# Second mixing one step further behind the first: a fused attention and gated feed-forward kernel in fp32

## The chip, the core and the metric

The kernel runs on one core of one Trainium2 chip. A core has five engines with a queue of instructions each: TensorE (PE, with its weight loads PEld), VectorE (DVE), ScalarE (ACT), GpSimd (POOL) and SyncE (SP, which here only starts transfers). Each engine works through its queue in order and waits on semaphores for the others. The metric is the device time of one launch in microseconds (us); lower is better.

## What is computed

Attention with two mixings over the heads, then a gated feed-forward block. Batch 4, 12 heads, 448 tokens, head size 64, everything in fp32.

```
scores = scale * np.matmul(q, k.transpose(0, 1, 3, 2))
scores = np.einsum('bhij,hg->bgij', scores, w_pre)      # first mixing
scores = scores - np.max(scores, axis=-1, keepdims=True)
attn = np.exp(scores)
attn = attn / (np.sum(attn, axis=-1, keepdims=True) + 1e-09)
attn = np.einsum('bhij,hg->bgij', attn, w_post)         # second mixing
x = np.matmul(attn, v)
...
xn = x / rms * rms_g
g = xn @ w_gate
out = (g / (1 + np.exp(-g)) * (xn @ w_val)) @ w_out     # 1792 tokens, 768 -> 1536 -> 768
```

## The kernel before

The first part (function `part_a`) is the attention, a software pipeline written out by hand. The queries of a batch are cut into four chunks, 16 chunks in all (`NCHUNK`); a chunk is worked in 6 steps, the last of each batch in 5 (`PAIRS`), which makes `T` = 92 steps. `first[n]` is the first step of chunk n. One step t does, in this order of issue:

- the transfers and small jobs due at t (`jobs_at`), among them in the steps of chunk 4 the reading of the first raw feed-forward weights: `fetch_w` starts a transfer into a ring of tiles with the tag "wraw", `first_w` issues one of five VectorE operations (lines 513 to 517) or the store of the result to `wf`;
- the first mixing `premix(t)` (line 182, tile `sp`, PSUM, contraction over 60 rows, a pair of 64-row halves), its matmuls alternating with those of one product of q and k for a later chunk (`qk_mm`, line 134, tile `qk`);
- `rowmax(t)` on VectorE (line 189, tile `nm`) and `expo(t)` on ScalarE (line 196, tile `e`, two tiles a step, with their sums `s`);
- the second mixing `postmix(t-1)` of the step before (line 223, tile `pm`), whose weights are the tiles `e` and whose moving operand is `wn`;
- the due units of the product with v (`av_mm`, line 267, from the table `av_at`), 16 short matmuls each;
- the copies of qk out of PSUM into `st` (lines 154 and 156) and the transfers that spread `st` over the rows of `r` (line 173), then the copies of pm into `at_all` (line 236 on VectorE, 238 on ScalarE);
- `norm(t)`: two small VectorE operations (`t` line 203, `rp` line 205) and on GpSimd `wn` (line 208), the mixing weights divided by the sums.

So `postmix(t-1)` stands in TensorE's queue after the first mixing of step t, and needs `wn` of t-1, which VectorE and GpSimd finish at the end of step t-1. GpSimd also adds and squares the results of the product with v (lines 290 to 305, tiles `xt` and `sum`, one operation a step, more towards the end).

In the last steps and for a few steps behind T, `extra` takes work of the second part into the pipeline: it loads x and the first weights again (`x_load`, `w_load`), splits each into a high and a low part (`x_split`, lines 577 and 578; `w_split`, line 684 on ScalarE and 685 on GpSimd, tile `wl`), and issues the first products (`both`, lines 600 to 602). What it takes in a step is decided by a budget of us per engine, `left`, which is smaller in steps in which a product with v is copied out (`done`). GpSimd also makes three tiles `d` (`diagonals`, line 358), which TensorE spreads over the partitions (`psy`, line 368). The second part (`part_b`) then is products of 128 by 128 weights with 448 columns, one behind the other, and is not touched by the change.

Tiles with one tag share a ring of `bufs` places; a write into a place waits until all readers of what stood there are done.

Of the kernel before, what the change touches and what calls it, by code (L numbers as in the profile page):

```python
# [7 lines left out]
F32 = mybir.dt.float32  # L8
# [37 lines left out]
def attention_moe(ctx: ExitStack, tc, q, k, v, wpre, wpost, mask, ident, wgv, wo, rms_g, out):  # L46
# [144 lines left out]
    def expo(n, p):  # L191
        sm[n, p] = pe.tile([128, 2], F32, name="s", tag="s")
        et[n, p] = []
        for u, ps in enumerate(sps.pop((n, p))):
            e = pe.tile([128, S], F32, name="e", tag="e", bufs=4)
            nc.scalar.activation(e, ps[:, :S], AF.Exp, bias=nmx.pop((n, p, u)), accum_out=sm[n, p][:, u : u + 1])  # L196
            et[n, p].append(e)

    def norm(n, p):
        k_ = halves_of(n, p)  # L200
        s = sm.pop((n, p))[:, :k_]
        t = pe.tile([128, 2], F32, name="t", tag="t")[:, :k_]
        nc.vector.tensor_scalar(t, s, 1e-9, None, ALU.add)
        r = pe.tile([128, 2], F32, name="rp", tag="rp")[:, :k_]
        nc.vector.reciprocal(r, t)  # L205
        wn[n, p] = pe.tile([128, 2, HR], F32, name="wn", tag="wn")
        for u in range(k_):
            nc.gpsimd.tensor_scalar(wn[n, p][:, u], wk, r[:, u : u + 1], 1.0, ALU.mult, ALU.mult)  # L208

    def postmix(n, p):  # L210
        ps = banks(ps_m, "pm")
        e, w = et.pop((n, p)), wn.pop((n, p))
        for u in range(2):
            u_ = min(u, len(e) - 1)
            for c in range(JC):
                for m in range(2) if c < JC - 1 else (u,):
                    j = min(2 * c + m, S // JT - 1) * JT
                    for v_ in range(2):
                        sl = slice(64 * v_, 64 * v_ + HR)
                        at_ = u * (JC - 1) + c if c < JC - 1 else JB - 1  # L220
                        o = ps[v_][64 * m : 64 * m + JT, : JB * HR].rearrange("p (s a i) -> p s a i", s=2, a=JB)
                        w_ = w[sl, u_].rearrange("p (s i) -> p s i", s=2)
                        nc.tensor.matmul(o[:, :, at_], e[u_][sl, j : j + JT], w_, start=True, stop=True)  # L223
        pm[n, p] = ps
# [155 lines left out]
    for i, a in enumerate([(n, hp) for n in range(1, NCHUNK) for hp in range(H // 2)][AHEAD:]):  # L380
        qk_at[i].append(a)
    for blk, ns in enumerate(BLOCKS):
        lo = first[ns[-1] + 1] + 1
        hi = first[ns[-1] + (3 if ns[-1] < 13 else 2)] + 1
        units = [(blk, i, part) for i in range(H // 2) for part in ((0, 1) if len(ns) > 1 else (None,))]
        for i, a in enumerate(units):
            t = lo + i * (hi - lo) // len(units)
            av_at[t].append(a)
            if ns[-1] % NC == NC - 1 and a[2] == 1:
                jobs_at[t + 1].append((load_v, ns[-1] // NC + 1, heads_of(blk)[a[1]]))  # L390

    def job(t, f, *a):
        jobs_at[t].append((f, *a))

    for n in range(NCHUNK):
        b, c = divmod(n, NC)
        if n > 2:
            for i in range(2):
                job(6 * n - 16 + 3 * i, load_q, n, 3 * i)
        for hp in range(H // 2):  # L400
            if n == 0:
                job(5 + 2 * hp, load_v, 0, heads_of(0)[hp])
        if n == 4:
            for i in range(4 * 7):
                job(first[n] + 4 + i, lambda i: first_w(i), i)
            for p in range(4):
                job(first[n] + 7 * p, lambda p: fetch_w(p), p)
    for t, todo_ in enumerate(list(qk_at)):
        for n, hp in todo_:
            if n % NC == NC - 1 and n + 1 < NCHUNK:  # L410
                job(t + 1, load_k, n // NC + 1, hp)
    for b in range(B - 1):
        t = first[NC * b + NC + 2] + (5 if b < B - 2 else 3)
        for i in range(17):
            last_at[t + max(i - 2, 0) // 3].append((sq_all, b, i))

    def part_a(extra):
# [29 lines left out]
        done = []  # L447
        for t in range(T + 24):
            def back(lag):
                return steps[t - lag] if 0 <= t - lag < T else None  # L450

            if t == first[NCHUNK - 1]:
                qk_ctx.close()
# [19 lines left out]
            if back(0):  # L473
                rowmax(*back(0))
                expo(*back(0))
            if back(1):
                postmix(*back(1))
            for a in av_at[t]:
                av_mm(*a)
            for a in qk_at[t][:1]:  # L480
                for j in range(2):
                    qk_evac(*a, j)
            if back(1):
                for v_ in range(2):
                    evac_a(*back(1), v_)
            if back(0) and t >= T - 2:
# [127 lines left out]
    conv = {}  # L614

    def fetch_w(p):
        raw = conv["raw", p] = pq.tile([128, 384, 2], I32, name="wraw", tag="wraw", bufs=3)
        src = wgv[0, :, 3 * p : 3 * p + 3].rearrange("p a f -> p (a f)").bitcast(I32)
        nc.sync.dma_start(raw.rearrange("p n t -> p (n t)"), src)

    def first_w(i):

        p, i = divmod(i, 7)
        if i < 5:
            if i == 0:
                conv["t"] = pq.tile([128, 2, 384], I32, name="wac", tag="wraw", bufs=3)
                conv[p] = to_f32(conv.pop(("raw", p)), *(conv["t"][:, j] for j in range(2)))
            conv[p][i]()
        elif i == 5:
            nc.sync.dma_start(wf[p // 2][:, (p % 2) * 384 : (p % 2) * 384 + 384], conv["t"][:, 1].bitcast(F32))  # L630
# [364 lines left out]
```

## Time and profile before

| | |
|---|---|
| time, median of 3 runs | 866.77 us (863.86, 866.77, 867.71) |
| the profiled execution | 866.41 us, its span 864.6 us |
| first steps to the last of the attention | about 21 to 346 us of the span |
| from there to the first product of the second part alone | 346 to 362 us |
| second part | 362.0 to 864.6 us |
| granted TensorE clock | 0.999 of full speed |

The span is what lies between the first and the last recorded instruction of the core; 1.8 us of the profiled time lie around it. A row of the profile names a line of the kernel, an engine, an operation and the tiles (out<-in), then how often, how long, and for how long the engine stood idle before it and what ended that. "issue" is idle time for which the profile shows no releaser. Matmuls overlap, and TensorE's busy share stays near 1 where short gaps between matmuls are covered by the modelled end of the one before; the gaps then show in the weight loads (PEld), which are issued in the same order.

### The profile page before, as it was taken

To read this page: it belongs to the slowest core of one execution; us is meant where nothing else is said; L and a number is where in the kernel's file an instruction comes from. 1 tells how busy PE (TensorE), PEld (TensorE's weight loads), DVE (VectorE), ACT (ScalarE), POOL (GpSimd) and SP (SyncE) were. 2 spreads that over 40 slices of the span, in tenths; PEclk is the share of its full clock that TensorE was granted. 3 is DMA by queue.
4 is the path that set the end of the run, shared out by engine and by line. 5 is a ranking of instruction groups with operands and counts; after the bars stand their busy time and mean duration, and the time that the engine had idled before them with its cause. 6 is when DMAs were issued, how large, how long until landed. Compare 5 with 4: busy or idle time off the path is not lost.

```text
span 864.6 us, 26550 instructions
## 1 busy us (share of the span) xinstructions
PE 827.3 (96%) x10900; PEld 710.8 (82%) x10900; DVE 600.4 (69%) x985; ACT 390.4 (45%) x869; POOL 437.6 (51%) x537
## 2 busy tenths in 40 slices
PE   7899999998899898999999999999999999999998
PEld 2556777777678686799999999999999999999997
DVE  5676787887677666778655858576668359978461
ACT  3677777777677676732211222222121235554310
POOL 7233455554555347935634646365356369573100
PEclk9999999999999999999999999999999999999999
DMA  7777678667756653744634535535354246664541
GB/s 203 202 229 206 202 226 237 213 196 220 223 156 178 184 165 111 231 155 118 215 100 153 139 119 154 179 98 170 105 180 138 64 134 195 201 189 134 170 129 64
DMA packets 77547, 144.53 MB, mean 167 GB/s; under 512 B 10495, under 2 KB 66845, under 8 KB 77427
## 3 DMA queue, kind: packets, MB, share of 16 engines
q1 hardware_dynamic: 72814, 129.19, 49.0%
q0 software_dynamic: 3648, 11.31, 4.8%
q10 hardware_dynamic: 965, 2.34, 0.8%
q8 instruction: 86, 1.41, 0.7%
q14 instruction: 34, 0.28, 0.1%
HBM read 72.03 MB, written 31.21 MB: 119 GB/s over the span
## 4 chain that ended last, share of the span: by engine, by line
PE 90%; DMA 3%; issue 3%; POOL 2%; DVE 1%; ACT 0%; ACTq 0%; SPq 0%; POOLq 0%; DVEq 0%
PE pm L223 9%; PE qk L134 8%; PE sp L182 7%; PE av L267 7%; PE pg L608 6%; PE pg L609 6%; PE pv L609 6%; PE pg L610 6%; PE pv L610 6%; PE pv L608 6%; PE po L610 6%; PE po L609 6%; PE po L608 6%; DMA r<-st 3%; POOL d L358 0%
## 5 line engine op out<-in xcount | busy, mean ns | idle before, releaser
L182 PE MATMUL sp<-r,wk_pre 64*64 64x448 f32 x720 | 162.7, 539 | 4.4 <-DMA r<-st 2.0
L134 PE MATMUL qk<-k,q 64*64 64x448 f32 x768 | 154.6, 560 | 5.9 <-DMA q<-in_q 4.1
L196 ACT ACTIVATE e<-sp,nm 128x448 f32<-128x448 f32 x180 | 114.4, 638 | 88.4 <-DVE nm L189 86.2
L223 PEld LDWEIGHTS pm<-wn,e 60*64 60x64 f32 x5152 | 110.1, 134 | 50.9 <-POOL wn L208 21.5
L189 DVE TENSOR_REDUCE nm<-sp 128x1 f32<-128x448 f32 x180 | 111.5, 622 | 56.2 <-PE sp L182 25.3
L208 POOL TENSOR_SCALAR wn<-wk,rp 128x60 f32<-128x60 f32 x180 | 55.8, 322 | 162.4 <-DVE rp L205 143.1
L223 PE MATMUL pm<-wn,e 60*64 60x60 f32 x5152 | 109.5, 220 | 18.0 <-issue 14.9
L267 PE MATMUL av<-at_all,v 64*64 64x240 f32 (+4 forms) x1728 | 95.1, 319 | 3.6 <-issue 3.6
L608 PE MATMUL pg<-x,wh 128*128 128x448 f32 x264 | 96.8, 367 | 0.0
L609 PE MATMUL pv<-x,wh 128*128 128x448 f32 x264 | 96.4, 365 | 0.0
L608 PE MATMUL pv<-x,wh 128*128 128x448 f32 x264 | 96.4, 365 | 0.0
L610 PE MATMUL pg<-x,wl 128*128 128x448 f32 x264 | 96.4, 365 | 0.0
L610 PE MATMUL pv<-x,wl 128*128 128x448 f32 x264 | 96.4, 365 | 0.0
L609 PE MATMUL pg<-x,wh 128*128 128x448 f32 x264 | 96.4, 365 | 0.0
L595 DVE TENSOR_TENSOR x<-hraw,x 128x448 fp32r<-128x448 f32 x84 | 91.6, 1137 | 6.8 <-ACT x L594 6.8
L609 PE MATMUL po<-x,fac 128*128 128x448 f32 x252 | 92.1, 365 | 0.0
L608 PE MATMUL po<-x,fac 128*128 128x448 f32 x252 | 92.0, 365 | 0.0
L610 PE MATMUL po<-x,fac 128*128 128x448 f32 x252 | 92.0, 365 | 0.0
L642 POOL TENSOR_TENSOR sg<-sg,u 128x448 f32<-128x448 f32 x36 | 48.1, 1335 | 83.0 <-DVE u L638 43.5
L637 ACT ACTIVATE sg<-g 128x448 f32<-128x448 f32 x48 | 27.4, 571 | 129.2 <-DVE g L636 118.6
L182 PEld LDWEIGHTS sp<-r,wk_pre 64*64 64x64 f32 x720 | 62.4, 133 | 22.2 <-issue 9.6
L638 DVE TENSOR_TENSOR u<-pv,ry 128x448 f32<-128x448 f32 x48 | 29.9, 623 | 69.1 <-PE pv L610 60.6
(118 smaller groups left out, 1709.9 us busy)
## 6 DMA issues: line engine op xcount, KB each, us to landing
r<-st SPq DMA_DIRECT2D x117, 210.0 KB
hraw<-td SPq DMA_DIRECT2D x84, 224.0 KB
wraw<-in_wgv SPq DMA_DIRECT2D x20, 768.0 KB
td<-keep SPq DMA_DIRECT2D x48, 224.0 KB
wraw<-in_wo SPq DMA_DIRECT2D x12, 768.0 KB
r<-st SPq DMA_DIRECT2D x44, 175.0 KB
v<-in_v SPq DMA_DIRECT2D x24, 256.0 KB
q<-in_q POOLq DMA_DIRECT2D x28, 192.0 KB, 5.1
```

The lines of the kernel that those rows point to most:

```text
L134: nc.tensor.matmul(ps[j][m, :S], qt[n][sl, hp, m], kt[n // NC, hp][sl], start=True, stop=True)
L182: nc.tensor.matmul(o, wk_pre[sl], rt[n][sl, 2 * p + v_], start=True, stop=True)
L189: nc.vector.tensor_reduce(t, ps[:, :S], AX.X, ALU.max, negate=True)
L196: nc.scalar.activation(e, ps[:, :S], AF.Exp, bias=nmx.pop((n, p, u)), accum_out=sm[n, p][:, u : u + 1])
L208: nc.gpsimd.tensor_scalar(wn[n, p][:, u], wk, r[:, u : u + 1], 1.0, ALU.mult, ALU.mult)
L223: nc.tensor.matmul(o[:, :, at_], e[u_][sl, j : j + JT], w_, start=True, stop=True)
L267: nc.tensor.matmul(x, vt[b, hp][sl, j, c_], a, start=(c_ == 0), stop=(c_ == JC - 1))
L595: nc.vector.tensor_tensor(lo, raw, hi.bitcast(F32), ALU.subtract)
L608: nc.tensor.matmul(ps, a, xh[:, kk], start=(kk == 0), stop=False)
L609: nc.tensor.matmul(ps, a, xl_[:, kk], start=False, stop=False)
L610: nc.tensor.matmul(ps, a2, xh[:, kk], start=False, stop=(kk == KT - 1))
L642: nc.gpsimd.tensor_tensor(h, sg, u, ALU.mult)
```

## The change

The second mixing of a step is issued two steps behind the first one, not one: `back(2)` where `back(1)` stood. After the last first mixing, in step T, both mixings that are left are issued one behind the other. The units of the product with v and the sums of squares (`sq_all`) go one step later with it, but for the last chunk. For this, six tiles `e` are kept in place of four. To make room, `t` and `rp` have three places in place of five, and the raw weights two in place of three, so that a raw tile is fetched every 9 steps, not every 7, each behind the store of the one before.

```
-            e = pe.tile([128, S], F32, name="e", tag="e", bufs=4)
+            e = pe.tile([128, S], F32, name="e", tag="e", bufs=6)
...
-        t = pe.tile([128, 2], F32, name="t", tag="t")[:, :k_]
+        t = pe.tile([128, 2], F32, name="t", tag="t", bufs=3)[:, :k_]
-        r = pe.tile([128, 2], F32, name="rp", tag="rp")[:, :k_]
+        r = pe.tile([128, 2], F32, name="rp", tag="rp", bufs=3)[:, :k_]
...
-        lo = first[ns[-1] + 1] + 1
-        hi = first[ns[-1] + (3 if ns[-1] < 13 else 2)] + 1
+        lag = 2 if ns[-1] < NCHUNK - 1 else 1
+        lo = first[ns[-1] + 1] + lag
+        hi = first[ns[-1] + (3 if ns[-1] < 13 else 2)] + lag
...
-            for i in range(4 * 7):
-                job(first[n] + 4 + i, lambda i: first_w(i), i)
             for p in range(4):
-                job(first[n] + 7 * p, lambda p: fetch_w(p), p)
+                for i in range(6):
+                    job(first[n] + 9 * p + 4 + i, lambda i: first_w(i), 7 * p + i)
+                job(first[n] + 9 * p, lambda p: fetch_w(p), p)
...
-        t = first[NC * b + NC + 2] + (5 if b < B - 2 else 3)
+        t = first[NC * b + NC + 2] + (6 if b < B - 2 else 4)
...
-                return steps[t - lag] if 0 <= t - lag < T else None
+                return steps[t - lag] if 0 <= t - lag < T and not t > T else None
...
-            if back(1):
-                postmix(*back(1))
+            late_ = [back(2)] if back(2) else []
+            for a in late_:
+                postmix(*a)
             for a in av_at[t]:
                 av_mm(*a)
...
-            if back(1):
+            for a in late_:
+                for v_ in range(2):
+                    evac_a(*a, v_)
+            if t == T:
+                postmix(*back(1))
                 for v_ in range(2):
                     evac_a(*back(1), v_)
...
-        raw = conv["raw", p] = pq.tile([128, 384, 2], I32, name="wraw", tag="wraw", bufs=3)
+        raw = conv["raw", p] = pq.tile([128, 384, 2], I32, name="wraw", tag="wraw", bufs=2)
...
-                conv["t"] = pq.tile([128, 2, 384], I32, name="wac", tag="wraw", bufs=3)
+                conv["t"] = pq.tile([128, 2, 384], I32, name="wac", tag="wraw", bufs=2)
```

TensorE's queue at the second step of the pipeline, before (`sp` is a first mixing, two rows of it a step; `pm` a second mixing):

```order
L182 MATMUL sp<-r_119,wk_pre 64x448 x2
L134 MATMUL qk<-k_0_126,q_238 64x448 x2
L182 MATMUL sp<-r_119,wk_pre 64x448 x2
L134 MATMUL qk<-k_0_126,q_238 64x448 x2
L223 MATMUL pm<-wn,e 64x2x30 x28
L182 MATMUL sp<-r_119,wk_pre 64x448 x2
```

The same place now:

```order
L182 MATMUL sp<-r_119,wk_pre 64x448 x2
L134 MATMUL qk<-k_0_126,q_238 64x448 x2
L182 MATMUL sp<-r_119,wk_pre 64x448 x2
L134 MATMUL qk<-k_0_126,q_238 64x448 x2
L182 MATMUL sp<-r_119,wk_pre 64x448 x2
L134 MATMUL qk<-k_1_128,q_238 64x448 x2
L182 MATMUL sp<-r_119,wk_pre 64x448 x2
L134 MATMUL qk<-k_1_128,q_238 64x448 x2
L223 MATMUL pm<-wn,e 64x2x30 x28
L182 MATMUL sp<-r_119,wk_pre 64x448 x2
```

The first second mixing stands behind three first mixings in place of two, and so it stays for all steps: what `pm` reads was made one step earlier.

GpSimd's queue in the last steps before T and behind it, before (`wl` are the low parts of the first weights; the `wn` of 128x60 without x2 is that of the last step):

```order
L208 TENSOR_SCALAR wn<-wk,rp 128x60 x2
L304 TENSOR_TENSOR xt_7226<-xt_7226 128x240
L305 TENSOR_TENSOR sum_6957<-sum_6957,xt_7226 128x240
L685 TENSOR_TENSOR wl<-wf,wh 128x384
L208 TENSOR_SCALAR wn<-wk,rp 128x60
L297 TENSOR_TENSOR xt_7328<-xt_7327 128x240
L302 TENSOR_TENSOR sum_6957<-xt_7328 128x120
L290 TENSOR_TENSOR xt_7485<-xt_7485,xt_7486 128x240
L297 TENSOR_TENSOR xt_7486<-xt_7485 128x240
L304 TENSOR_TENSOR xt_7486<-xt_7486 128x120
L685 TENSOR_TENSOR wl<-wf,wh 128x384 x3
```

GpSimd's queue now, two pieces of it, the first from four steps ahead of T:

```order
L691 TENSOR_TENSOR wl<-wf,wh 128x384 x2
L304 TENSOR_TENSOR xt_7082<-xt_7082 128x240
L305 TENSOR_TENSOR sum_6979<-sum_6979,xt_7082 128x240
L208 TENSOR_SCALAR wn<-wk,rp 128x60 x2
```

```order
L290 TENSOR_TENSOR xt_7361<-xt_7361,xt_7362 128x240
L691 TENSOR_TENSOR wl<-wf,wh 128x384
L208 TENSOR_SCALAR wn<-wk,rp 128x60
L304 TENSOR_TENSOR xt_7261<-xt_7261 128x240
L305 TENSOR_TENSOR sum_6979<-sum_6979,xt_7261 128x240
L691 TENSOR_TENSOR wl<-wf,wh 128x384
```

Of the four `wl`, one stood ahead of the last `wn` and three behind it; now three stand ahead, two of these some steps earlier, and one behind. The budget moved them: the copies of the product with v come a step later, and another step has the larger budget.

## Rows read from the trace of the kernel before

**Rows 1.** The page: busy time and instructions by engine; the chain by engine.

```profile
PE 827.3 (96%) x10900; PEld 710.8 (82%) x10900; DVE 600.4 (69%) x985; ACT 390.4 (45%) x869; POOL 437.6 (51%) x537
...
PE 90%; DMA 3%; issue 3%; POOL 2%; DVE 1%; ACT 0%; ACTq 0%; SPq 0%; POOLq 0%; DVEq 0%
```

**Rows 2.** Stretches: length; busy us of PE, PEld, DVE, ACT, POOL; clock; DMA, GB/s.

```profile
64.20:320.30 256.10, 239.38 (x6458) 191.31 (x6450) 190.09 (x462) 183.74 (x486) 125.28 (x269) 1.00 0.67 201
326.60:340.40 13.80, 11.69 (x425) 9.04 (x419) 9.92 (x22) 9.43 (x26) 11.04 (x24) 1.00 0.31 99
340.40:346.30 5.90, 4.58 (x195) 3.62 (x186) 2.57 (x8) 3.36 (x11) 4.84 (x9) 1.00 0.24 65
346.30:362.00 15.70, 14.22 (x238) 11.19 (x232) 12.94 (x14) 11.59 (x26) 15.38 (x18) 1.00 0.77 229
362.00:864.60 502.60, 498.77 (x2460) 461.18 (x2460) 338.23 (x381) 142.71 (x228) 247.76 (x158) 1.00 0.47 145
```

**Rows 3.** Lines in 64 to 320: count, busy us, mean ns, idle before, releasers.

```profile
L223 PEld LDWEIGHTS pm<-wn,e 60*64 60x64 f32 x4037 | 88.1, 134 | 34.2 <-issue 15.5 <-POOL wn L208 11.5 <-DVE nm L189 0.2
...
L267 PEld LDWEIGHTS av<-at_all,v 64*64 64x64 f32 x1248 | 57.4, 133 | 5.9 <-issue 5.6
...
L182 PEld LDWEIGHTS sp<-r,wk_pre 64*64 64x64 f32 x565 | 52.7, 133 | 15.9 <-issue 8.3 <-ACT e L196 3.9 <-ACT at_all L238 2.4
...
L134 PEld LDWEIGHTS qk<-k,q 64*64 64x64 f32 x576 | 45.2, 132 | 8.3 <-ACT st L156 1.3 <-issue 1.2 <-PE pm L223 0.5
...
L154 DVE COPY st<-qk 128x448 f32<-128x448 f32 x73 | 44.8, 614 | 0.0
```

**Rows 4.** Chain of waits, steps 194 to 203: start us, us, what.

```profile
194.34 0.80 PE pm L223 x49
...
197.38 0.79 PE pm L223 x43
...
200.52 0.50 PE pm L223 x26
...
201.01 1.53 issue
```

**Rows 5.** Timeline of one step: start us, us, engine, work, [idle before].

```profile
204.63 1.38 DVE L189 TENSOR_REDUCE nm<-sp 128x1 f32<-128x448 f32 x2 [0.39 <-PE qk L134]
...
207.22 0.17 DVE L205 RECIPROCAL rp<-t 128x2 f32<-128x2 f32 x1
...
207.56 0.60 POOL L208 TENSOR_SCALAR wn<-wk,rp 128x60 f32<-128x60 f32 x2 [1.07 <-DVE rp L205]
...
207.93 1.11 PEld L223 LDWEIGHTS pm<-wn,e 60*64 60x64 f32 x50 [0.22 <-POOL wn L208]
```

**Rows 6.** Who waited for whom, whole span: us, times, longest.

```profile
PEld pm L223 <- POOL wn L208: 21.5, 56, 1.6
...
PEld pm L223 <- issue: 21.3, 36, 2.3
```

**Rows 7.** The same, weight loads alone, 326 to 363.

```profile
PEld pm L223 <- POOL wn L208: 6.1, 6, 1.6
PEld psy L368 <- POOL d L358: 1.4, 1, 1.4
PEld pv L602 <- POOL wl L685: 1.2, 1, 1.2
```

**Rows 8.** Timeline of POOL, 338 to 363.

```profile
347.38 3.70 POOL L685 TENSOR_TENSOR wl<-wf,wh 128x384 fp32r<-128x384 f32 x3
...
359.46 0.66 POOL L302 TENSOR_TENSOR sum<-xt 128x100 f32<-128x100 f32 x1
...
360.65 1.31 POOL L358 TENSOR_TENSOR d<-eye,y 112x448 f32<-112x448 f32 x1
```

**Rows 9.** The page: DMA queue, packets, MB, share.

```profile
q8 instruction: 86, 1.41, 0.7%
```

## Prediction, made before the changed kernel ran

> **What bounds the kernel now.** I read the page first. TensorE holds 90% of the chain that ended last, "issue" 3%, GpSimd 2% [rows 1]. So the question is where TensorE stands still in the attention. The busy times by stretch come next [rows 2]: from 362.0 us on TensorE is busy 498.77 of 502.60 us, and no edit is there, so all of a gain must come from the first 362 us. From 64.2 to 320.3 us, the regular steps, TensorE shows 239.38 of 256.10 us busy, VectorE 190.09, ScalarE 183.74 and GpSimd 125.28: TensorE is nearest to full, and the others have room. From 346.3 to 362.0 us GpSimd takes over with 15.38 of 15.70 us. The granted clock is 1.00 in all five stretches, so the clock plays no part.
>
> Then the waits. The weight loads of the second mixing waited 21.5 us in 56 waits for GpSimd's `wn`, and 21.3 us in 36 waits for nothing that the profile shows [rows 6]. The timeline of one step shows how the first kind arises: VectorE begins `rowmax` at 204.63 and ends `rp` at 207.39 (207.22 + 0.17), 2.76 us later; GpSimd starts `wn` at 207.56, and the weight loads of pm go at 207.93 after 0.22 us of idleness [rows 5]. That chain through VectorE, ScalarE and GpSimd is as long as a step, so `wn` comes just when TensorE asks for it. The changed order asks one step later, and this wait goes.
>
> **How much of the wait is in the time.** A weight load that waits is not an array that stands still: the last matmuls of qk still run. So I go by the step. There are 73 steps in the 256.1 us (73 copies st<-qk) [rows 3], 3.51 us each. Of the idle time of the weight loads there, 15.5 + 5.6 + 8.3 + 1.2 = 30.6 us are "issue" [rows 3], which the change doesn't address. Without it a step takes (256.1 - 30.6)/73 = 3.09 us. The chain shows a step without any wait: pm starts at 194.34 and again at 197.38, 3.04 us [rows 4]. The difference, 0.05 us x 73 = 3.6 us, is what all waits on other engines cost together. The upper bound is the whole 11.5 us that pm waits for `wn` in this stretch, the lower one 0. The waits on ScalarE (`e` 3.9, `at_all` 2.4, `st` 1.3 us, same rows) stay, so I take 3 us, just under the 3.6.
>
> **The change part by part.**
>
> The head of the pipeline: of the 21.5 us, 11.5 are in the regular steps and 6.1 in the last ones [rows 3, 7], so 3.9 us are left, nearly all in the first steps, where there is no product with v yet. There VectorE's 2.76 us of work a step [rows 5] is longer than TensorE's own, and it becomes the bound as soon as the wait goes. Bounds 0 and 3.9 us; I take 1.
>
> The last four steps before T-1, 326.6 to 340.4 us, take 13.8 us, and `wn` holds pm in all four; from there to 346.3 us it holds two more (6.1 us in six waits [rows 7]). Four steps at 3.04 us would be 12.2 us, a gain of 1.6. GpSimd is the next bound: it is busy 11.04 of the 13.8 us [rows 2], and two `wl` come in here as the queue shows, each 3.70/3 = 1.23 us as measured further on [rows 8], which makes 13.5 us. It need not be done in each step any more, as pm asks a step later, but it must not fall further and further behind. Bounds 0.3 (13.8 - 13.5) and 1.6 plus the excess of the four waits, about 4; I take 1.7.
>
> T-1 to the second part, 340.4 to 362.0 us: GpSimd's work is 4.84 + 15.38 = 20.2 of 21.6 us [rows 2], and TensorE's last wait is for `d` (1.4 us), an earlier one for `wl` (1.2 us) [rows 7]. Two of the four `wl` leave this stretch, 2 x 1.23 = 2.5 us, and one addition to `sum` (0.66 us [rows 8]) now stands behind the last `d`: 3.1 us less ahead of the end at 361.96 us (360.65 + 1.31). TensorE's own waits here are those 1.4 and 1.2 us and two of the six for `wn`, 2 us at their mean of 6.1/6: 4.6 us that it could give. Against it: in T two second mixings stand one behind the other, the second writes the same two PSUM tiles as the first and must wait until these are copied out (0.58 us on VectorE by the same copy [rows 5], and about as long on ScalarE), and a unit of the product with v comes behind T. Bounds 0 and 4.6; I take 2.6, GpSimd's 3.1 less one such copy.
>
> Added at no cost: six tiles `e` and the smaller rings cost no instruction. With six, `expo(t)` overwrites what the mixing of step t-3 read, done a whole step before. The same number of instructions runs on every engine. In the ring of two, a fetch of raw weights waits on SP's queue for VectorE's last reading and stands behind the store of the piece before; queued behind both are the transfers r<-st, for which first mixings wait. Three fetches and four stores are concerned; 0 if the operation is done, at most a step each, 3 x 3 us, if VectorE lags; these operations run in earlier steps, so 0.
>
> Sum: 3 + 1 + 1.7 + 2.6 = 8.3 us off the profiled 866.41 us gives 858.1; I say 858. The profiled execution lies 0.4 us under the median of 866.77, so the two are one for this purpose.
>
> **Code or data.** The waits called "issue" stand inside runs of pm, where nothing is waited for: at 201.01 us the run breaks off for 1.53 us [rows 4]. There are 10,900 matmuls and 10,900 weight loads [rows 1], and queue q8, of the kind instruction, moved 86 packets with 1.41 MB [rows 9], one for some 250 instructions. I read these waits as TensorE running out of loaded code; the profile doesn't name it. The Trainium skill (page "Runtime: NRT & Kernel Launch", section "Instruction fetch mechanics") states that code comes in blocks of 256 instructions and that the cost of crossing into the next is "mostly hidden". The count agrees; "hidden" doesn't agree with breaks of 1.53 and up to 2.3 us. By that rule the third and the fourth case below would have no ground, and the sum would stay 858.
>
> **The rivals.**
>
> (1) The wait is covered anyway. For it: the step loses only 0.05 us to all waits together, and the end of the attention has GpSimd at 15.38 of 15.70 us. Then only the three `wl` help: 2.5 us at most, and 866.4 - 2 = 864 to 865. Against it: six waits of 6.1 us in the last steps, with nothing on TensorE to cover them.
>
> (2) Slower: more breaks for code. A TensorE that is no longer held at `wn` runs through its loaded instructions sooner, and the first pm that is left out shifts where in a step a block ends. Place: the regular steps, pm and av, whose breaks are 15.5 + 5.6 = 21.1 us now. If two thirds as much came on top, 14 us, the time would be 866.4 - 8.3 + 14 = 872. It decides from 8.3 us on, and beyond the 0.5% from 8.3 + 4.3 = 12.6 us. Against it: the number of instructions and their order within a step stay.
>
> (3) Both kinds of waiting shrink, since TensorE's queue, no longer held at pm, runs ahead further and asks for the next code sooner. With half of the 21.1 us and a sum as above, 866.4 - 8.3 - 10 = 848; with a quarter 853.
>
> (4) The change doesn't do what it says, since pm stays held by something else. The queue shows it one step later throughout, and the PSUM tiles that it writes are copied out in the step before, as now. I give it no chance of its own; it would look like (1).
>
> **How the numbers follow.** The forecast, 858 with its own range of 854 to 862.5, gets 0.60; (1) 0.19; (2) 0.08; (3) 0.13. About 0.5%, 4.3 us, is what a measurement of this kernel can tell from no change. Faster: nearly all of the forecast (0.57) and (3), 0.70. Within: (1) and the edge of the forecast (0.03), 0.22. Slower: 0.08. The range for 8 in 10 reaches from the upper part of (3) into (1): 850 to 865.
>
> **What would show it.** In the profile after: pm's wait for `wn` falls from 21.5 us to under 4; the regular steps without breaks come to 3.04 to 3.06 us; the "issue" sum of pm stays at 21 us, give or take 6; the second part alone begins at 353 to 355 us, not 362.0, and its 502.6 us stay; three `wl` run before the last `wn`, and TensorE's wait for `d` is below 2 us. Wrong would be: a step of 3.09 us or more without breaks while the wait for `wn` is gone (then another wait took its place: `sp` on `e`, or at_all), an "issue" sum above 33 us, or a start of the second part after 358 us.

## The result: no gain, and the profile after

The changed kernel takes 868.21 us (median of 22 runs, 861.24 to 873.80), the kernel before 862.63 us in the same set (22 runs, 854.26 to 871.16): a ratio of 1.0075, 95% interval 1.005 to 1.010. I had said 858 with a range of 850 to 865.

One set is not the last word on it. The kernel before was timed in seven more sets and the changed kernel in two. The means of the sets of before lie between 862.7 and 867.6 us, those of after between 865.8 and 868.5 us. Over all of them it is 865.5 us (149 runs) against 867.2 us (45 runs): 1.7 us slower, 0.2%. (Five slow executions, over 1.5% above the fastest of their kernel, are left out of these means, and the trace of b_again below is of one of them.) What is to be explained is a gain of 8.3 us that did not come. A loss isn't shown: the 1.7 us are less than the 4.9 us by which the sets of before differ among themselves, and in the other two sets of the changed kernel its ratio is 0.9998 (0.9966 to 1.0031) and 0.9983 (0.9954 to 1.0012).

The page of the changed kernel, its busy times by engine and the chain by engine, answers to [rows 1]; the same number of instructions runs, and TensorE holds the chain as before:

```profile
PE 828.5 (96%) x10900; PEld 719.5 (84%) x10900; DVE 599.8 (70%) x985; ACT 389.8 (45%) x869; POOL 438.4 (51%) x537
...
PE 91%; DMA 3%; POOL 2%; issue 2%; DVE 1%; ACT 1%; ACTq 0%; SPq 0%; POOLq 0%; DVEq 0%
```

The waits of the weight loads over the whole span, with sum, count and longest, answer to [rows 6]:

```profile
PEld pm L223 <- issue: 21.4, 50, 2.1
PEld sp L182 <- ACT e L196: 9.3, 32, 1.5
...
PEld pm L223 <- POOL wn L208: 5.0, 18, 1.2
```

The wait for `wn` fell from 21.5 us in 56 waits to 5.0 in 18. The change does what it says. "issue" is where it was, 21.4 against 21.3 us.

The busy times by stretch (length; PE, PEld, DVE, ACT, POOL; clock; DMA, GB/s), cut at the steps t = 14, 84, 91 and at the last of the six `psy` loads ahead of the second part, answer to [rows 2]:

```profile
66.55:308.67 242.12, 229.34 (x6243) 189.18 (x6238) 184.70 (x449) 177.95 (x472) 119.53 (x257) 1.00 0.69 207
308.67:333.52 24.85, 23.34 (x733) 20.69 (x724) 16.64 (x41) 17.96 (x48) 18.40 (x38) 1.00 0.53 164
333.52:356.71 23.19, 21.11 (x507) 17.09 (x502) 17.11 (x24) 16.41 (x38) 21.73 (x29) 1.00 0.55 163
356.71:859.50 502.79, 498.78 (x2460) 461.06 (x2460) 337.30 (x379) 140.35 (x225) 248.05 (x159) 1.00 0.47 144
```

The second part begins at 356.7 us in this trace and at 362.1 in that of before, which looks like a gain of 5.4 us. It is none: this trace is of the shortest execution of its set (861.24 us), the one of before (866.41 us) of a long one. So both kernels were run and traced again, twice each, and the stretches of all six traces set side by side.

How the table is made: a step begins with its first weight load of `sp`. "Breaks" are stretches of over 0.25 us from the start of one weight load to the start of the next that end at one place in every 256 of TensorE's instructions (a load and its matmul counted as two, a semaphore instruction as one; of 96 such stretches over 0.6 us between t=14 and t=84 in the six traces, 78 end at 192 to 195 beyond a multiple of 256). "Half" is time from t=14 to 84 at a granted clock of 0.50, that is 1.2 GHz. "Net" is t=14 to 84 less the breaks and less half of that time, which is what work at half the rate costs at most.

| us | t=0 to 14 | 14 to 84 | breaks | half | net | 84 to 91 | 91 to last psy | second part |
|---|---|---|---|---|---|---|---|---|
| before | 47.5 | 246.8 | 25.2 | 0 | 221.6 | 25.1 | 21.7 | 502.5 |
| b_again | 48.7 | 249.1 | 25.4 | 10.2 | 218.6 | 25.1 | 22.2 | 505.1 |
| b_r2 | 46.8 | 242.2 | 17.9 | 3.4 | 222.6 | 25.0 | 22.2 | 502.6 |
| after | 45.5 | 242.1 | 19.6 | 0 | 222.5 | 24.9 | 23.2 | 502.7 |
| a_again | 43.3 | 242.9 | 20.1 | 0 | 222.8 | 24.7 | 23.2 | 502.5 |
| a_r2 | 47.0 | 245.6 | 20.9 | 6.1 | 221.6 | 24.8 | 23.0 | 502.8 |

Four things stand in it, b_again left aside. The regular steps, net, gained nothing: 221.6 and 222.6 against 222.5, 222.8 and 221.6 us. The head lost 1.9 us of its time on the mean (47.1 to 45.3), with 3.4 us at half clock in the head of after not taken out. The end, from t=84 to the last `psy`, grew by 0.9 us (47.0 to 47.9). And breaks and half clock differ by 7 and 6 us between executions of one kernel, more than anything that the change moves.

### The profile page after: what moved, and what is told of

The parts are those of the page before. It is cut to its first block, busy times and chain, and to the rows that moved or that the text cites. A ratio compares the mean times of both kernels' runs of the same rounds, so it can differ in the third digit from the quotient of the medians.

```text
span 859.5 us, 26557 instructions
## 1 busy us (share of the span) xinstructions
PE 828.5 (96%) x10900; PEld 719.5 (84%) x10900; DVE 599.8 (70%) x985; ACT 389.8 (45%) x869; POOL 438.4 (51%) x537
## 4 chain that ended last, share of the span: by engine, by line
PE 91%; DMA 3%; POOL 2%; issue 2%; DVE 1%; ACT 1%; ACTq 0%; SPq 0%; POOLq 0%; DVEq 0%
PE pm L223 9%; PE qk L134 8%; PE sp L182 8%; PE av L267 7%; PE pg L614 6%; PE pv L616 6%; PE pg L616 6%; PE pg L615 6%; PE pv L615 6%; PE pv L614 6%; PE po L614 6%; PE po L615 6%; PE po L616 6%; DMA r<-st 2%; DMA q<-in_q 1%
## 5 line engine op out<-in xcount | busy, mean ns | idle before, releaser
L223 PEld LDWEIGHTS pm<-wn,e 60*64 60x64 f32 x5152 | 116.2, 135 | 39.1 <-issue 21.4
L223 PE MATMUL pm<-wn,e 60*64 60x60 f32 x5152 | 111.8, 220 | 13.2 <-issue 11.4
L134 PEld LDWEIGHTS qk<-k,q 64*64 64x64 f32 x768 | 55.2, 135 | 29.6 <-issue 8.0
```

Of the source, the lines that this page charges most:

```text
L134: nc.tensor.matmul(ps[j][m, :S], qt[n][sl, hp, m], kt[n // NC, hp][sl], start=True, stop=True)
```

## The experiments

**Is it the head's clock?** The first trace of the changed kernel has 3.4 us at half clock in the head, from 42.6 us on, behind gaps of 1.99 and 1.15 us in its weight loads. Two variants of the changed kernel were to keep TensorE busier there, beside both kernels as they are. head_lag1 keeps the order of before for the first steps:

```
-            late_ = [back(2)] if back(2) else []
+            late_ = [back(1)] if 0 < t < 9 else [] if t == 9 else [back(2)] if back(2) else []
```

filler puts idle work into step 6:

```
+            if t == 6:
+                for _ in range(4):
+                    nc.tensor.matmul(busy[:, :S], ones, kt[0, 0], start=True, stop=True)
             sp = premix(*back(0)) if back(0) else []
```

> The kernel before once more, with a second trace and more times. Clock theory (the changed kernel loses time because TensorE falls to half its clock at its wait for r<-st near 42 us, and the kernel before does not): mean granted clock 0.998 or more in most executions, no stretch at half clock in the trace but the very end. Break theory (the loss is in the breaks of pm and av called issue, which differ from execution to execution): the clock like that of the changed kernel, and an issue sum of the weight loads in 64 to 320 us that differs from 30.6 us by more than 5.

> The changed kernel once more, with a second trace. Its first trace is of its fastest execution (861.24 us against a median of 868.21), so it hides the loss. Clock theory: mean clock 0.992 to 0.996, a stretch of 3 to 14 us at half clock that begins near 42 us, and by it the first regular step some 3 to 7 us later than in the kernel before; the regular steps 5 to 6 us shorter in all. Break theory: clock does not matter, the regular steps show 8 us more of issue than in the first trace.

> The changed kernel with the old distance of one step for the first eight second mixings; in step 9 none is issued, from step 10 on it is two. Only the head of the pipeline differs. Clock theory: the half clock goes as in the kernel before, and the median comes down by 4 to 8 us from the changed kernel's, to 860 to 864. Break theory: within 2 us of the changed kernel, since the regular steps are the same.

> The changed kernel with four more filler matmuls (ones by k, into a PSUM bank that nobody reads) at the head of step 6, in the wait for r<-st. Clock theory: TensorE is kept at work over the wait, no half clock, median 4 to 8 us below the changed kernel's. Break theory: the same or 1 us slower, as the four take 0.8 us each where TensorE does not wait.

Measured medians: b_again 864.37, a_again 866.28, head_lag1 865.16, filler 863.12 us, each 12 runs, with intervals of the ratio some 0.6% wide: none is told apart from another. b_again itself, the same kernel as its reference, has a ratio of 0.9973 (0.9942 to 1.0004). Half clock came in b_again too, 20 us of it before t=84. The suspicion fell: it strikes either kernel. What stands ahead of it is seen in b_r2, in windows and in the timeline of the loads:

```profile
80.00:84.90 4.90, 2.91 (x88) 2.08 (x82) 2.72 (x7) 3.29 (x9) 1.97 (x4) 1.00 0.71 230
85.00:88.40 3.40, 3.40 (x32) 2.53 (x26) 1.12 (x4) 0.53 (x1) 1.25 (x3) 0.50 0.72 242
88.40:92.00 3.60, 3.60 (x104) 2.84 (x99) 2.87 (x7) 2.89 (x8) 0.71 (x3) 1.00 0.38 132
```

```profile
84.27 0.37 PEld L223 LDWEIGHTS pm<-wn,e 60*64 60x64 f32 x18 [2.13 <-issue]
```

TensorE broke off for 2.13 us inside a run of pm, and then worked 3.4 us at 0.50 with 32 matmuls, where the 3.6 us behind it hold 104. Such a break alone doesn't do it: the trace of before has one of 2.3 us [rows 6] and no half clock ahead of the span's end.

**Does the wait cost anything where it stands?** b_nowait is the kernel before, with pm on `wk`:

```
-                        w_ = w[sl, u_].rearrange("p (s i) -> p s i", s=2)
+                        w_ = wk[sl].rearrange("p (s i) -> p s i", s=2)
```

> The kernel before, with one edit: the second mixing takes the mixing weights as they are (wk) and not wn. It leaves out the division by the sums; wn is still made, but nothing waits for it. So the wait that the change was to remove is gone, without a longer pipeline. Wait theory (my prediction's step): the 21 us of waits for wn are partly in the time; the regular steps from t=14 to t=84, without breaks and without time at half clock, fall from 218.6 - 221.6 us by 3 us or more, and the last steps from t=84 to the last psy from 46.8 - 47.3 us by 3 to 4 us. Full-array theory: a step of 3.03 us is what TensorE's own columns take, in the regular steps nothing falls (218 to 223 us); in the last steps, where GpSimd is nearly full, up to 2 us.

Net 222.9 us (235.9 less 13.0 of breaks): nothing. From t=84 to the last `psy` 48.3 us with 3.4 at half clock, so 46.6: at most 0.5 us. The median is 860.72 us, a ratio of 0.9944 (0.9899 to 0.9988), 3 us less than its set's 863.74; in the trace it is the breaks that are fewer, not the steps. So in the steps the wait for `wn` was covered. Whether the breaks are fewer because nothing waits for `wn` any more isn't shown: the one trace is of the fastest of six executions (855.26 us).

**By how much?** b_chain and a_chain write `wn` twice, so that it comes 0.6 us later:

```
+            for _ in range(2):
                 nc.gpsimd.tensor_scalar(wn[n, p][:, u], wk, r[:, u : u + 1], 1.0, ALU.mult, ALU.mult)
```

> The kernel before, with wn written twice by the same two GpSimd operations: the chain that ends in wn is 0.6 us longer in each of 92 steps, all else alike. Full-array theory: the wait in the kernel before is covered, but only by the matmuls still in the array; of 0.6 us more per step the part beyond that cover shows, 0.1 to 0.5 us a step, 8 to 45 us in all. Wait theory: every 0.6 us counts in full, 50 us. If the chain to wn were far from mattering: 0 to 2 us (the last steps, where GpSimd is full).

> The changed kernel with the same addition (wn written twice). Here the second mixing asks for wn a step later. If what the change buys is slack and not time: within 2 us of the changed kernel in the regular steps (t=14 to 84 without breaks 221 to 224 us), 1 to 3 us more in the last steps, since GpSimd is full there. If the change doesn't decouple the chain: as much slower as the kernel before with this addition.

Medians 880.76 (ratio 1.015, 1.0099 to 1.0202) and 873.78 us (1.0092, 1.0061 to 1.0124). Net 240.5 and 221.2 us: the kernel before pays 18 us, 0.26 us of each 0.6, the changed kernel nothing. The waits from 64 to 310 us, first of b_chain, then of a_chain:

```profile
PEld pm L224 <- POOL wn L209: 37.9, 61, 2.2
```

```profile
PEld pm L224 <- POOL wn L209: 2.3, 10, 0.4
```

So the change does decouple the chain, and what it buys is slack. In a kernel whose `wn` came 0.6 us later it would be worth 18 us of net steps; of the whole time it is 7.0 us here, the difference of the two medians. Of a_chain's 6.6 us over the changed kernel's 867.2 I can place only about 1 at the end; its trace holds 24.7 us of breaks and 10 us of half clock, which may be the rest.

**What fills the step?** a_pe issues one of the four matmuls of a product of q and k twice, a_dve one copy on VectorE:

```
+            for _ in range(2 if j and u and n > 1 else 1):
                 nc.tensor.matmul(ps[j][m, :S], qt[n][sl, hp, m], kt[n // NC, hp][sl], start=True, stop=True)
...
+            for _ in range(2 if n > 1 else 1):
                 nc.vector.tensor_copy(st, ps[:, :S])
```

> The changed kernel, with one of the four matmuls of each product of q and k (from chunk 2 on, 84 steps) issued twice, into the same place. In the trace one such matmul is two rows; rows of 448 columns take 0.54 us, of 240 columns 0.34, of 60 columns 0.22, so some 0.00083 us a column beside 0.17 us of passage. Full-array theory: a quarter of the array works 4 x 448 + 14 x 60 + 4 x 240 = 3592 columns a step, 3.0 us, which is the step of 3.03 us; 2 x 448 more columns on one quarter make 0.75 us more a step, 3.78 us, and about 60 us in all. If another engine set the step, with room on TensorE: 0 to 20 us.

> The changed kernel, with VectorE's copy of qk (0.61 us) made twice in the same 84 steps. Full-array theory: VectorE works about 2.6 us of a step of 3.03 us, so 0.61 us more makes it 3.2 us and VectorE sets the step: 0.2 us a step, some 15 us; up to 0.4 us of it is hidden. If VectorE's chain already set the step: 0.6 us a step, 50 us.

The undisturbed step (lower quartile of the 70) is 3.78 us in a_pe (median 3.83), what the count of columns says: 3.03 + 0.75. It is seen in the starts of `wn` on GpSimd, 3.8 to 3.9 us apart:

```profile
150.23 0.59 POOL L209 TENSOR_SCALAR wn<-wk,rp 128x60 f32<-128x60 f32 x2 [2.70 <-DVE rp L206]
154.11 0.60 POOL L209 TENSOR_SCALAR wn<-wk,rp 128x60 f32<-128x60 f32 x2 [1.59 <-DVE rp L206]
157.92 0.66 POOL L209 TENSOR_SCALAR wn<-wk,rp 128x60 f32<-128x60 f32 x2 [1.20 <-DVE rp L206]
```

The array was full. The count itself is less exact than it looks: a quarter of the rows of the product with v have 120 columns, not 240 (0.26 and 0.37 us a row in the changed kernel; the 0.34 of the expectation is their mean). So every second step has 3352 columns, 2.8 us, the others 3592, 3.0 us, and both kinds take 3.03 us. Yet the whole time grew by 36 us (899.56, ratio 1.0418), not by 60: the breaks fell to 4.3 us. The single waits called "issue" in a_pe (64 to 310 us) are short, where the changed kernel's go up to 2.1 us:

```profile
PEld sp L183 <- issue: 16.6, 96, 0.2
PEld pm L224 <- issue: 15.9, 66, 0.4
```

a_dve was a miss. I expected 3.2 us a step; it is 3.57, and 887.23 us (1.0288, 1.0217 to 1.0359). If VectorE sets that step, then without the added 0.61 us its turn is 2.96 us, hardly shorter than the array's 3.03. Its busy time, 190.09/73 = 2.60 us a step [rows 2, 3], doesn't show this: the waits inside its loop with TensorE and ScalarE belong to the turn. That a matmul more and a copy more both lengthen the step almost in full is also what a single loop through TensorE and VectorE would give. For the array speaks the chain of the kernel before, 93% of it on TensorE from 180 to 230 us (shown below); no run parts the two.

**With room in the array.** b_less and a_less leave out half of the product with v:

```
-        for c_ in range(JC) if part is None else (2 * part, 2 * part + 1):
+        for c_ in (1, 3) if part is None else (2 * part + 1,):
...
-                    nc.tensor.matmul(x, vt[b, hp][sl, j, c_], a, start=(c_ == 0), stop=(c_ == JC - 1))
+                    nc.tensor.matmul(x, vt[b, hp][sl, j, c_], a, start=(c_ == 1), stop=(c_ == JC - 1))
```

> The kernel before with half of the product with v left out (two of four pieces of the keys; the output is not the reference's). That takes 480 of 3592 columns a step from a quarter of the array, 0.4 us: the array would need 2.6 us. Full-array theory: here the chain to wn sets the step of the kernel before, since there is nothing left to cover the wait: 2.9 to 3.0 us a step without breaks, so little gain (5 to 12 us), and the wait for wn in the regular steps grows well above 11.5 us. If columns don't set the step: no gain and the same waits.

> The changed kernel with the same half of the product with v left out. Full-array theory: with room on the array the change brings what it could not bring in the full kernel: steps of 2.65 to 2.8 us without breaks, 10 to 20 us less than the kernel before with the same part left out. If the change has no use at all: the two within 3 us of each other.

855.42 against 854.82 us: no difference, a miss for my theory as I had put it. The undisturbed steps are 2.83 and 2.91 us. The loads' waits of b_less, then of a_less (80 to 300 us):

```profile
PEld pm L223 <- POOL wn L208: 23.3, 58, 1.6
...
PEld sp L182 <- ACT e L196: 8.5, 39, 0.7
```

```profile
PEld sp L182 <- ACT e L196: 12.5, 48, 2.4
...
PEld pm L223 <- POOL wn L208: 5.3, 21, 0.3
```

One wait goes and the next stands there: `sp` for the PSUM tile that the exponential still reads. Array, the loop through VectorE and ScalarE, and the chain to `wn` lie within 0.2 us of each other; taking away one is worth nothing by itself.

**The end.** a_tail1 returns to the order of before at step 81, by issuing both second mixings that are due there. b_av1 is the kernel before with the product with v one step later, alone:

```
-        lag = 2 if ns[-1] < NCHUNK - 1 else 1
+        lag = 2 if ns[-1] < 13 else 1
...
-            late_ = [back(2)] if back(2) else []
+            late_ = [back(2)] if back(2) and t <= first[14] else [back(1)] if back(1) and t > first[14] else []
...
-            if t == T:
+            if t == first[14]:
                 postmix(*back(1))
...
```

> The changed kernel up to step 81, where both second mixings that are due are issued one behind the other, and from there the order of the kernel before (second mixing one step behind, units of the product with v as before from chunk 12 on). Drain theory: the changed kernel loses 1 to 1.5 us from t=91 to the last psy (23.2 us against 21.7 - 22.2), since one more second mixing and one more unit of the product with v stand there, and they were not issued earlier anywhere; here that stretch goes back to 21.7 - 22.2 us, and the second mixing that is issued twice in step 81 lengthens t=70 to 84 by 0.7 to 1.5 us; the whole time as the changed kernel within 1 us. If the loss comes from the smaller rings or six tiles e: 23.2 us stay.

> The kernel before, with only the units of the product with v and the sums of squares one step later, as in the change; the second mixing stays one step behind. Drain theory: one more unit of the product with v behind T-1 costs its columns, 8 matmul rows of 240 columns on a quarter of the array, 8 x 240 x 0.00083 = 1.6 us if TensorE is full there, less what its waits there leave: t=91 to the last psy 22.3 to 23.5 us against 21.7 to 22.2. If only the second mixing in T makes the drain longer: 21.7 to 22.2 us.

a_tail1: t=91 to the last `psy` is 22.1 us again, TensorE busy for 18.91 of it where the changed kernel has 21.11:

```profile
345.71:367.81 22.10, 18.91 (x428) 14.92 (x420) 15.46 (x22) 15.59 (x36) 20.71 (x27) 1.00 0.62 185
```

Step 81 pays for it: 6.34 us, of it 1.66 us of a break, and 1.25 us ahead of the second pm, which writes the tiles of the first; without the break some 1.7 us more than a step. Its net sum of 228.1 us is some 6 above the changed kernel's; beside step 81 the trace shows one wait of 2.52 us for `e`, and the rest stays open. Median 869.82 us (1.0073, 1.0036 to 1.0109): no version to keep. b_av1: 864.99 us (1.0000, 0.9960 to 1.0039). From t=84 to the last `psy` it takes 49.5 us with 3.4 at half clock, so about 47.8, as the changed kernel's 47.9; but 2.8 us of it are one wait for `wn` before t=91, and behind t=91 it is 22.0 us. So one more unit of the product with v behind T-1 doesn't make that stretch longer by TensorE's columns, as the expectation had it: TensorE is busy 20.43 us in it, 1.6 more than in b_r2, and it takes no longer. From t=91 to the last `psy`, b_r2 and then b_av1:

```profile
335.08:357.28 22.20, 18.85 (x428) 14.92 (x419) 15.61 (x22) 15.42 (x37) 20.81 (x27) 1.00 0.62 184
340.64:362.66 22.02, 20.43 (x459) 16.71 (x451) 14.97 (x20) 13.99 (x32) 21.16 (x27) 0.95 0.60 165
```

The last number ahead of the clock is GpSimd's. It is busy for all of this stretch but 1.4 us, in a_tail1 too (20.71 of 22.10) and in the changed kernel (21.73 of 23.19), and the last `psy` waits for its last `d`:

```profile
PEld psy L368 <- POOL d L358: 1.3, 1, 1.3
```

That row is of the changed kernel; the kernel before has 1.4 us [rows 7]. The length of this stretch is GpSimd's work. In b_av1 alone GpSimd is idle less, 0.9 us.

The repetition of both kernels for the table:

> The kernel before, once more, to have a further trace of it and its time beside that of the changed kernel in one set. Drain and full-array theories: t=14 to 84 without breaks and half clock 218 to 222 us, t=84 to 91 25.1 us, t=91 to the last psy 21.7 to 22.2 us.

> The changed kernel, once more. Drain and full-array theories: t=14 to 84 without breaks and half clock as b_r2 within 2 us, t=84 to 91 24.7 to 25.2 us, t=91 to the last psy 23.2 us, 1 to 1.5 us more than b_r2; the median 1 to 2 us above b_r2, with breaks that differ by some us from execution to execution on top. A further cause in the regular steps or the head (code, half clock): 4 us or more above b_r2.

862.77 and 866.74 us, ratios of 0.9973 (0.9938 to 1.0008) and 0.9983 (0.9954 to 1.0012) to their common reference, so 0.1% apart where the medians are 4 us apart. From t=91 to the last `psy` it is 0.75 us more, less than the 1 to 1.5 expected; a further cause of 4 us in the steps isn't seen in the table.

**Fewer instructions?** Since breaks take 18 to 25 us and fell in a_pe, three kernels cut TensorE's instructions: pm with weights of 128 keys in place of two with 64.

```
-                for m in range(2) if c < JC - 1 else (u,):
+                for m in (0,) if c < JC - 1 else (u,):
+                    wide = 2 if c < JC - 1 else 1
...
-                        nc.tensor.matmul(o[:, :, at_], e[u_][sl, j : j + JT], w_, start=True, stop=True)
+                        nc.tensor.matmul(o[:, :, at_], e[u_][sl, j : j + JT * wide], w_, start=True, stop=True)
```

> The kernel before, with two neighbouring matmuls of the second mixing (64 keys each, same moving operand) made one with 128 keys: 16 in place of 28 a step, the same results in the same places, a half of the array for one in place of a quarter. Columns for a quarter stay 14 x 60; matmul and weight rows of TensorE go from 176 to 128 a step. Theory that breaks come from the number of instructions: the floor stays 3.03 us, the breaks from t=14 to 84 fall from 18 - 25 us to 5 - 12, the whole time by 8 to 20 us. If breaks have nothing to do with the number: breaks and time as before within 3 us. If loading weights of 128 columns takes longer than two of 64 beside each other: slower, 0.1 to 0.3 us a step.

> The changed kernel with the same edit. Full-array theory: as b_wide in the regular steps within 2 us, and 1 us more at the end; the change then still buys nothing. If the change only failed since breaks covered the waits: 4 to 8 us less than b_wide.

> As b_wide, and the products of q and k in the same way: two matmuls with 128 queries in place of four with 64, so 120 rows a step. Theory of the number: a further 0 to 4 us less than b_wide. Against it: a product of q and k then holds a half of the array, while a first mixing that stands between wants a quarter of it; if that costs, the step grows by 0.1 to 0.4 us, up to 30 us in all.

943.48 (1.0882, 1.0852 to 1.0912), 940.81 (1.0853, 1.0823 to 1.0883) and 1091.94 us (1.2583, 1.2546 to 1.2619). The breaks did fall, to 1.4 and 1.8 us in b_wide and a_wide, but a step takes 4.36 us. The merged matmuls still start two at a time, 0.007 us apart, but a pair starts only every 0.112 us, where four of the small ones start every 0.057 us in the kernel before. So 24 rows of them take 1.77 us in b_wide. Their weight loads take 0.187 us each, against 0.134 for 64 columns; that these are the cause, one of the cases I had named, wasn't tested, and of the 1.33 us that a step grew not all is placed. With wide products of q and k as well a step takes 6.19 us.

```profile
199.80 1.77 PE L224 MATMUL pm<-wn,e 60*128 60x60 f32 x24
```

b_wide and a_wide have next to no breaks and no half clock up to the span's end, and so are the cleanest comparison of the change: t=0 to 14 takes 52.6 us in b_wide and 50.1 in a_wide, t=14 to 84 310.5 in both, t=84 to the last `psy` 54.7 and 55.0. In all the change is 2.7 us faster there by the medians (six runs each), and it is the head that is left of it; I had expected it 1 us slower. And they hold a warning. The loads' waits from t=14 to 84, b_wide and then a_wide:

```profile
PEld pm L224 <- POOL wn L208: 38.8, 55, 0.7
```

```profile
PEld pm L224 <- POOL wn L208: 40.2, 57, 0.7
```

In a_wide `wn` is made a whole step ahead, and the row blames it as before. The name is that of the last semaphore event; what the load waits for is something else, by all that stands above the array.

## Why the prediction was wrong, step by step

**Regular steps, -3 us: failed.** I took 3.09 us (steps less "issue") against 3.04 (one step without a wait), and put the difference of 0.05 x 73 down to waits on other engines. The same division gives 3.11 us for the changed kernel, (242.12 - 24.3)/70 with 24.3 us of "issue" in its loads, where the wait for `wn` is nearly gone: the 0.05 was not that wait. The step of 3.03 us is the array: 4 x 448 + 14 x 60 + 4 x 240 columns at 0.00083 us are 3.0 us (2.8 in every second step), a_pe adds 0.75 and gets 3.78, b_nowait takes the wait away and its net steps gain nothing. The trace of before had shown it. This is its chain from 180 to 230 us by line:

```profile
by line: PE pm L223 25.6%; PE av L267 23.7%; PE sp L182 22.1%; PE qk L134 21.6%; issue 7.6%
```

TensorE's own work and "issue" fill it, and `wn` isn't in it. I had written "A weight load that waits is not an array that stands still" and then counted part of it all the same. 23 of the 70 steps of before take under 3.06 us, 22 of after.

**Head, -1 us: right in sign.** It is 1.9 us by the table and 2.5 by the wide pair. But much of it may be work put off: one second mixing and one unit of the product with v fewer stand in the head, and they come back at the end. b_av1, which puts off the product with v alone, has 45.7 us there; b_nowait, which puts off nothing and has no wait for `wn`, has 45.7 too. So how much of the head was wait and how much is work put off stays open.

**Last four steps before T-1, -1.7 us: failed.** t=84 to 91 went from 25.1 to 24.8 us, and b_nowait, where nothing waits for `wn`, has 25.1: the waits here were covered too. My four steps at 3.04 us were too low a floor. One of the four, t=88, has two units of the product with v where the others have one, and takes 4.09 us in the kernel before; the four steps from t=87 on, 13.8 us, take 13.9 to 14.0 in the changed kernel. What holds them isn't shown: the rows of the product with v have 120 columns and fewer in most of them, and the count of columns comes to some 10 us. It is not the wait that I priced.

**T-1 to the second part, -2.6 us: failed, and this is the step that turned the sign.** That GpSimd bounds this stretch was right: in all six traces of the table the last `psy` begins 0.16 us behind the end of GpSimd's last `d`, and from t=91 to there GpSimd is idle for 1.4 to 1.5 us only. What failed is the size of its work. I priced it at 3.1 us less, and one copy of 0.58 us against that. It is busy 20.3 and 20.8 us in before and b_r2 and 21.7, 21.7 and 21.5 us in the three traces of the changed kernel: 1.1 us more on the mean, and the stretch grew by as much, from 21.7 - 22.2 to 23.0 - 23.2 us. The two `wl` did leave (4.8 us for four became 2.0 for two). But the operations on `xt` and `sum` grew from 12.1 to 15.7 us, since additions and squares of the late product with v came in, which I had not counted. TensorE's work grew too: it was busy 4.58 + 14.22 = 18.80 us there [rows 2] and is now 21.11, by one second mixing and the unit of the product with v behind T that I named without a price. That filled its waits and not the time, as b_av1 shows. (Rows of the last two chunks have at most 120 columns, so that such a unit is some 0.7 us of columns, not the 1.6 that the expectation of b_av1 counts with 240.) What came in on GpSimd stands ahead of the last `wn`:

```profile
335.29 1.21 POOL L290 TENSOR_TENSOR xt<-xt,xt 128x480 f32<-128x480 f32 x1
336.58 0.99 POOL L297 TENSOR_TENSOR xt<-xt 128x480 f32<-128x480 f32 x1
337.53 1.16 POOL L290 TENSOR_TENSOR xt<-xt,xt 128x240 f32<-128x240 f32 x1
338.65 0.99 POOL L691 TENSOR_TENSOR wl<-wf,wh 128x384 fp32r<-128x384 f32 x1
339.62 0.31 POOL L208 TENSOR_SCALAR wn<-wk,rp 128x60 f32<-128x60 f32 x1
```

The mixing of T-1 waits for it, in the timeline of the loads of the same kernel:

```profile
339.99 0.43 PEld L223 LDWEIGHTS pm<-wn,e 60*64 60x64 f32 x20 [1.19 <-POOL wn L208]
```

**Edits at no cost: right.** No wait on the raw weights or the smaller rings shows in the changed kernel's rows.

**Rivals.** (1), the wait is covered, is what happened; I gave it 0.19, with 2 us of gain from the `wl` that didn't come. (2) and (3) did not come: "issue" stayed at 21 us. What I had called 0.5% for a measurement is fair, but sets of one kernel differ by as much, 862.7 to 867.6 us, so the first set's 5.6 us is less sure than its interval says.

**The signs I had named.** Right: "issue" at 21.4 us, the second part's 502.8, three `wl` ahead of the last `wn`, TensorE's wait for `d` at 1.3 us. Missed: 5.0 us of waits for `wn` (under 4), and 356.7 us for the second part (353 to 355), which by itself would have passed for half a success; it is 362.4 us in a_r2. Missed as well is the step without breaks: 3.11 us by my own division, not 3.04 to 3.06. That is a sign of being wrong that I had named, 3.09 us or more with the wait for `wn` gone. I had read it as another wait in its place; it is TensorE's own work.

**What stays open.** By the table the head's -1.9, the end's +0.9 and the net steps' +0.2 (with half clock only roughly taken out) make -0.8 us, and the wide pair says -2.7; the runs say +1.7. The difference is within the spread of breaks and clock, and was not placed. So no loss is shown, and of the gain at most the head's.

## What to carry to other kernels

Before a wait is priced, count what the array itself needs in a step; where that is the step, a wait in its weight loads is covered, and taking it away buys slack, which pays only once something else gets later. A deeper pipeline puts work off: what its head saves, its end must do, so price the postponed work there, on the engine that the end waits for (here GpSimd), and not only the waits that go. And compare stretches over several executions before a gain is read from a pair of traces.

## What the runs showed of the hardware that I had not expected

Most of TensorE's breaks (78 of 96 over 0.6 us) come at one place in every 256 of its instructions, and they take 18 to 25 of some 245 us in the two kernels. They went to 4.3 us and to 1.4 us where a step gave the array more time for the same or for fewer instructions (a_pe, b_wide). The Trainium skill (page "Runtime: NRT & Kernel Launch", section "Instruction fetch mechanics") calls the crossing "mostly hidden"; in those two kernels that agrees, in the two of this case it doesn't.

Matmuls with 64 rows and 64 columns fill the four quarters of the array side by side: all rows of a step one behind the other would be some 11.5 us by the count of columns, and a step takes 3.03. Those of the second mixing run in fours, one such group every 0.057 us. Merged to 128 columns they run in pairs, one pair every 0.112 us, and a step takes 4.36 - 3.03 = 1.33 us more.
